# Moving sums to VectorE, norms half a group earlier and w_out blocks apart in the MLP stage of a fused attention, MoE and relu² kernel

## The chip, the cores and the metric

The kernel runs on one core of one Trainium2 chip. The metric is device time in microseconds of one execution, from the runs of a set. A NeuronCore has TensorE (PE; matmul), VectorE (DVE), ScalarE (ACT), GpSimd (POOL) and SyncE (SP), which each go through their instructions in order and meet at semaphores. PSUM holds what TensorE writes, SBUF the rest. [...]

## The reference

The kernel does three things one after the other, on 2304 tokens of 512 numbers: causal windowed attention with ALiBi, a top-1 mixture of experts, and an MLP whose activation is the square of relu. The change is in the third:

```python
def _moe2_ref(x, w_in, w_out):
    h = x @ w_in          # (2304, 512) @ (512, 2048)
    r = np.maximum(h, 0.0)
    g = r * r
    return (g @ w_out)    # (2304, 2048) @ (2048, 512)
```

## The kernel before

The last stage, `moe2`, begins at about 413 us. Its tokens are taken as they lie after the experts, in nine groups G of 256 (two tiles of 128 tokens). The output is put in the right order at the end, by an indirect scatter of each tile.

For a group there are three kinds of work.

- `norm(G)` scales the group's rows. It is a generator, so its steps can be placed between other work: ACT takes the absolute value (L1110), PE sums it (L1115), DVE makes the scale (L1118 to L1124), PE spreads it (L1129), DVE multiplies (L1130); then four differences of blocks of x (L1137 to L1140, on DVE for groups below 5, on POOL behind that) and the split of all blocks into two fp16 parts (casts L1150 on ACT, rests L1152 or L1156 on DVE). norm(G+2) is made while group G is at work.
- `wide1(G, m)` makes one half m of x @ w_in by a Strassen scheme: seven products of 24 matmuls (L1176). ACT takes the results out of PSUM (`keep`, L1188) and DVE joins them (L1189, L1221, L1223). `square(i)` makes relu² of them: on DVE for groups 0 to 2 (L1201), on ACT for 3 to 8 (L1204, L1205). `halves` splits a block of g into two fp16 parts, by a cast on ACT (L1195) and a subtraction on DVE (L1196).
- The product with w_out. Groups 0 to 2 are plain (SG = 3): `wide2(G, m)` takes 48 matmuls of 512 columns (L1351 to L1353) per half. Groups 3 to 8 use a Strassen scheme here as well: `seven(G, part)`, with products of 12 matmuls of 256 columns (L1307), eight in part 0 and six in part 1. It needs sums of blocks of g (L1208 and L1212 on POOL, L1214 and L1216 on DVE) and combined blocks of w_out.

Those combined blocks, for eight k, are made by `mix(k)`, which is a generator too. Its first call makes two sums (L1272) and four differences (L1274 to L1277) of a block on POOL, in scratch space: a column of `yT` that is free, or `dec`. Its second call splits them by ACT casts (L1281) and DVE (L1282). The table MIXES gives, at each of the points at(G, 0) to at(G, 4) between the halves, the blocks that begin or finish there: a block's first mention begins it, its second finishes it.

The order on each engine is made by a scheduler in the recording framework, which keeps to dependencies and to hints: `issue_after` puts what is recorded in it behind a given instruction, `behind` does so for one instruction. `end_act` and `end_dve` are the last `halves` of ACT and DVE. The outer loop is in `moe2`: wide2(G, 0) or seven(G, 0), wide1(G+1, 0), wide2(G, 1) or seven(G, 1), wide1(G+1, 1), with calls of `step()` (one step of norm(G+2)) and at(...) between.

In the profiled execution wide1(1,0) starts at 437.6 us, wide1(2,0) at 478.0, wide1(4,0) at 571.05, and seven(8,1), the last work, ends at 769.4.

Of the kernel before, what the change touches and what calls it, by code (L numbers as in the profile page):

```python
# [16 lines left out]
ALU = mybir.AluOpType  # L17
# [29 lines left out]
GT = 2  # L47
GW = GT * P
SG = 3
SCRATCH = {0: 0, 1: 1, 2: 1, 4: 3, 7: 4}  # L50
MIXES = {(0, 4): (0,), (0, 0): (1,), (0, 1): (0,), (0, 2): (1,), (1, 4): (2, 3), (1, 1): (2, 3),
         (2, 4): (4, 5), (2, 1): (4, 5), (2, 2): (7, 6), (2, 3): (7, 6)}
STEPS = (((2, 6), ()), ((1, 5), (1,)), ((4,), (1,)), ((1, 5), (1,)), ((1, 5), (1,)), ((3,), (1, 3)), ((3,), (1, 3)),
         ((1, 3, 5, 7), (1, 3)))
SPARE = ((), (), (4, 5, 6, 7), (4, 5, 6, 7), (4, 5, 6, 7), (6, 7), (7,), ())
# [38 lines left out]
class K:  # L94
    def __init__(self, ctx, tc, q, k, v, wg, w1, w2, wi, wo, cst, pad, out):
        self.ctx, self.tc, self.nc = ctx, tc, tc.nc
        self.q, self.k, self.v, self.wg, self.w1, self.w2, self.wi, self.wo, self.cst, self.pad, self.out = \
            q, k, v, wg, w1, w2, wi, wo, cst, pad, out
        self.cp = ctx.enter_context(tc.tile_pool(name="cp", bufs=1))
        self.wr = ctx.enter_context(tc.tile_pool(name="wr", bufs=12))  # L100
        self.rw = ctx.enter_context(tc.tile_pool(name="rw", bufs=4))
        self.ps = ctx.enter_context(tc.tile_pool(name="ps", bufs=2, space=PSUM))
        self.yp = ctx.enter_context(tc.tile_pool(name="yp", bufs=1))
        self.ep = ctx.enter_context(tc.tile_pool(name="ep", bufs=2))
        self.dr = ctx.enter_context(tc.tile_pool(name="dr", bufs=1, space=DRAM))
        self.xts, self.fac, self.gts = {}, {}, {}
        self.turns, self.narrow = 0, False
        self.wt = {}

        self.yT = self.yp.tile([P, 4, YC], F32, name="yT")  # L110
        self.xd = self.dr.tile([N, 2 * DM], F16, name="xd")
        self.ids = self.dr.tile([E * N + P, 2], F32, name="ids")
        self.cols = self.dr.tile([YC + P, 2], F32, name="cols")
        self.wod = self.dr.tile([P, 8 * 2 * DM], F16, name="wod")
# [1065 lines left out]
    def wide1(self, G, m, between=lambda k: None):  # L1180


        nc, V = self.nc, self.nc.vector
# [14 lines left out]
        def square(i):  # L1198
# [6 lines left out]
            nc.scalar.activation(ci, ci, AF.Square, scale=0.5)  # L1205
            both = lambda t: (t[:, a].rearrange("p (o j n) -> p o j n", o=2, j=4) for a in range(2))
            if i == 0:
                nc.gpsimd.tensor_tensor(p1, c[:, :, 0, 0], c[:, :, 0, 1], op=ALU.subtract)  # L1208
                halves(*(t[:, 0] for t in both(g[3])), c[:, :, 0, 0])
                halves(*(t[:, 1] for t in both(g[3])), p1)  # L1210
                return
            nc.gpsimd.tensor_tensor(p5, c[:, :, 0, 1], c[:, :, 1, 1], op=ALU.add)  # L1212
            halves(*(g[0][:, a].rearrange("p (j n) -> p j n", j=4) for a in range(2)), ci)
            V.tensor_tensor(u, p5, c[:, :, 0, 0], op=ALU.subtract)  # L1214
            halves(*both(g[1]), self.part(22528, 8 * P).rearrange("p (o j n) -> p o j n", o=2, j=4))
# [34 lines left out]
    def mix(self, k):  # L1250
# [10 lines left out]
            x = [pair(d[:, :512]), pair(d[:, 512:])]  # L1261
        if k < 2:
            y = [xg().bitcast(F16).rearrange("p (o a n) -> p o a n", o=2, a=2) for _ in range(2)]
        elif k < 6:
            col = column(k - 2).bitcast(F16).rearrange("p o (a n) -> p o a n", a=2)
            y = [col[:, 0:2], col[:, 2:4]]
        else:
            y = [self.wo_pair[f].rearrange("p (o a d) -> p o a d", o=2, a=2)[:, :, :, GW:] for f in (((0, 2), (4, 6))[k - 6])]
        self.wt[k] = [y[o // 2][:, o % 2] for o in range(4)]
        for o in range(2):  # L1270
            w = self.wo_s[8 * o + k]
            Q.tensor_tensor(x[o], *(w[:, a].rearrange("p (o n) -> p o n", o=2) for a in range(2)), op=ALU.add)  # L1272
        t1, t3, t4, t2 = (x[o // 2][:, o % 2] for o in range(4))
        Q.tensor_tensor(t1, t3, t1, op=ALU.subtract)  # L1274
        Q.tensor_tensor(t3, t2, t3, op=ALU.subtract)
# [54 lines left out]
    def put(self, G, i, o, src=None):  # L1330
        nc = self.nc
        if src is not None:
            self.end_act = nc.scalar.activation(o, src, AF.Copy, scale=self.fac[G][:, 1, i:i + 1])  # L1333
        k = G * GT + i
        nc.gpsimd.indirect_dma_start(  # L1335
            out=self.out, out_offset=bass.IndirectOffsetOnAxis(ap=self.oid[:, k:k + 1], axis=0),
            in_=o, in_offset=None)

    def wide2(self, G, m, then=lambda i: None):
        nc = self.nc  # L1340
# [19 lines left out]
    def moe2(self):  # L1360
# [15 lines left out]
        def at(*key):  # L1376
            for n in MIXES.get(key, ()):
                if n in mixing:
                    for _ in mixing.pop(n):
                        pass  # L1380
                else:
                    mixing[n] = self.mix(n)
                    next(mixing[n])

        mixing = {}
        for G in range(NG):
# [4 lines left out]
                with tc.issue_after(self.end_act.ins), tc.issue_after(self.end_dve.ins):  # L1391
                    next(nr)

            at(G, 4)
            if G < SG:
                self.wide2(G, 0)
            else:
                self.seven(G, 0, lambda k: step() if k in (5, 7) else None)
            at(G, 0)
            if more:  # L1400
                self.wide1(G + 1, 0, lambda k: step() if G >= SG and k < 2 else at(G, 1) if k == 1 else None)
            if G < SG:
                step()
                self.wide2(G, 1, lambda k: step() if k != 1 else None)
                if G + 1 == SG:
                    self.narrow = True
            else:
                self.seven(G, 1, lambda k: step() if k == 3 else None)
            at(G, 2)
            if more:  # L1410
                self.wide1(G + 1, 1, lambda k: step() if G >= SG and k == 0 else None)
# [61 lines left out]
```

## Time and profile before

| | us |
|---|---|
| three runs | 777.4, 782.7, 784.3 |
| median of them | 782.7 |
| the profiled execution | 782.7 |
| its span | 780.8 |
| busy in the span: PE | 718.3 (92%) |
| DVE | 592.3 (76%) |
| ACT | 443.3 (57%) |
| POOL | 236.2 (30%) |

The span is what the profiler recorded from first to last instruction; the execution's time has 1.9 us more around it. Busy time is the sum of an engine's instructions. A row of a timeline gives the start, the length, the engine, the line of the kernel, the operation, what it writes and reads, and in brackets how long its engine stood before it and what it waited for. A row of waits gives the instruction that waited, the one it waited for, the total, how often, and the longest.

### The profile page before, as it was taken

The page shows a single profiled execution, that of the slowest core. Times are in us where ns is not written, and L with a number is a line of the kernel's source. Part 1 is how long each engine was busy: PE and PEld are TensorE (multiplying, and loading weights), DVE is VectorE, ACT ScalarE, POOL GpSimd, SP SyncE. Part 2 cuts the span into 40 slices and gives each one's busy share as a digit, 9 for nine tenths or more (in the row PEclk, how much of TensorE's full clock was granted, in tenths as well). Part 3 has the DMA queues.
Part 4 walks back from the last instruction along what each step waited for, and adds up shares of the span by engine and source line. Part 5 has one row for each costly group of instructions (what it writes and reads, how often), then busy time and mean ns, then how long its engine had stood idle before and what let it go on. Part 6 is the DMA issues. An engine that isn't in the chain of part 4 may idle for free. (4 is left out here: it accounts for less than half of the span.)

```text
span 780.8 us, 19641 instructions
## 1 busy us (share of the span) xinstructions
PE 718.3 (92%) x7979; PEld 601.6 (77%) x7979; DVE 592.3 (76%) x1430; ACT 443.3 (57%) x748; POOL 236.2 (30%) x271
## 2 busy tenths in 40 slices
PE   6889999997979899998898999998799999999995
PEld 5889899787636566787797777675689898989994
DVE  5898889855679998887798987867567777777672
ACT  5878898733456565656533333336456565656561
POOL 4583421534632010000003453444622222222121
PEclk9999999999999999999899999999889999999998
DMA  9796215766789785476404000000000000000000
GB/s 339 275 387 151 65 56 135 240 173 158 244 292 299 239 258 172 153 244 223 155 31 138 1 29 2 28 2 28 1 2 29 2 29 3 29 2 29 2 29 28
DMA packets 35656, 91.71 MB, mean 117 GB/s; under 512 B 5209, under 2 KB 13547, under 8 KB 35547
## 3 DMA queue, kind: packets, MB, share of 16 engines
q1 hardware_dynamic: 29803, 75.77, 30.4%
q0 software_dynamic: 5760, 14.65, 5.7%
q8 instruction: 64, 1.05, 0.6%
q14 instruction: 29, 0.24, 0.1%
HBM read 77.54 MB, written 13.04 MB: 116 GB/s over the span
## 5 line engine op out<-in xcount | busy, mean ns | idle before, releaser
L1176 PEld LDWEIGHTS <-wi 128*128 128x128 f16 x3024 | 170.5, 98 | 8.8 <-issue 7.3
L1307 PEld LDWEIGHTS <-wr 128*128 128x128 f16 x1008 | 99.2, 99 | 20.1 <-ACT wr L1195 4.4
L1195 ACT CAST wr<-work 128x1024 f16<-128x1024 f32 (+1 forms) x72 | 59.9, 832 | 77.6 <-DVE work L1201 44.5
L1176 PE MATMUL ps_b<-work,wi 128*128 128x128 f16 x1368 | 85.5, 219 | 4.4 <-ACT work L1188 2.9
L1196 DVE TENSOR_TENSOR wr<-work,wr 128x1024 f16<-128x1024 f32 (+1 forms) x72 | 74.7, 1051 | 15.3 <-ACT wr L1195 13.1
L850 PE MATMUL ps_c<-work,wr 128*128 128x352 f16 (+5 forms) x256 | 75.0, 297 | 10.8 <-DVE work L799 9.8
L849 PE MATMUL ps_c<-work,wr 128*128 128x352 f16 (+5 forms) x256 | 75.0, 297 | 8.2 <-ACT yT L852 6.3
L1176 PE MATMUL ps_a<-work,wi 128*128 128x128 f16 x1248 | 78.2, 219 | 0.0
L851 PE MATMUL ps_c<-work,wr 128*128 128x352 f16 (+5 forms) x256 | 75.0, 297 | 0.0
L310 PE MATMUL ps_a<-yT,wr 128*128 128x192 f32 (+2 forms) x288 | 64.2, 342 | 6.8 <-DMA wr<-in_q_dram 5.2
L322 ACT ACTIVATE pb<-pb,nm 128x192 f32<-128x192 f32 (+2 forms) x144 | 56.1, 432 | 12.6 <-DVE nm L315 11.8
L770 DVE SCALAR_TENSOR_TENSOR wr<-rw,wr 128x1024 f16<-128x1024 f32 x40 | 48.7, 1220 | 6.4 <-ACT wr L769 6.4
L769 ACT ACTIVATE wr<-rw 128x1024 f16<-128x1024 f32 x40 | 42.1, 1057 | 19.1 <-DMA rw<-in_w_dram 18.6
L1272 POOL TENSOR_TENSOR yT<-wr 128x512 f32<-128x512 f16 x6 | 10.5, 1753 | 136.6 <-ACTq L1064 123.3
L310 PEld LDWEIGHTS ps_a<-yT,wr 128*128 128x128 f32 x288 | 45.0, 198 | 8.0 <-DMA yT<-in_k_dram 6.3
L315 DVE CUSTOM_DVE_ANT_0 pb<-ps_a,bias 128x192 f32<-128x192 f32 (+2 forms) x144 | 44.2, 326 | 8.8 <-PE ps_a L310 8.4
L1335 POOL DMA_INDIRECT out_dram<-o,oid x18 | 19.6, 1088 | 100.1 <-ACT o L1333 84.8
L851 PEld LDWEIGHTS <-wr 128*128 128x128 f16 x288 | 29.4, 102 | 21.5 <-issue 14.4
L1204 ACT ACTIVATE work<-work 128x1024 f32<-128x1024 f32 x24 | 25.3, 1055 | 34.0 <-DVE work L1189 34.0
L333 PE MATMUL ps_b<-cst,pb 128*128 128x128 f32 x256 | 43.7, 281 | 0.5 <-ACT pts L337 0.4
L850 PEld LDWEIGHTS <-wr 128*128 128x128 f16 x288 | 29.4, 102 | 17.6 <-issue 10.2
L778 POOL DMA_INDIRECT xg<-xd,idx x21 | 24.3, 1158 | 51.6 <-PE ps_d L786 40.8
(297 smaller groups left out, 1921.7 us busy)
## 6 DMA issues: line engine op xcount, KB each, us to landing
rw<-in_w_dram SPq DMA_DIRECT2D x40, 512.0 KB, 5.7
wi<-in_w_dram SPq DMA_DIRECT2D x20, 512.0 KB, 6.5
rw<-in_wo_dram SPq DMA_DIRECT2D x16, 512.0 KB, 3.9
rw<-in_wi_dram SPq DMA_DIRECT2D x32, 256.0 KB, 5.3
wr<-in_q_dram SPq DMA_DIRECT2D x14, 512.0 KB, 8.5
xd<-xhl POOLq DMA_DIRECT2D x16, 256.0 KB, 5.3
yT<-in_k_dram SPq DMA_DIRECT2D x7, 576.0 KB, 10.7
rw<-in_v_dram SPq DMA_DIRECT2D x12, 325.0 KB, 5.6
```

Of the source, the lines that this page charges most:

```text
L310: nc.tensor.matmul(ps[:, s, first:hi], q[g, u, hh // 4][:, hh % 4, s if u < 4 else 0, :], self.kt[g, hh // 2][:, hh % 2, key0:key0 + hi - ...
L315: self.last_ttr = nc.vector.tensor_tensor_reduce(out=pb[:, s, first:hi], in0=ps[:, s, first:hi], in1=self.bias[:, hh, first - lo:192], sca ...
L322: self.last_exp = nc.scalar.activation(pb[:, s, first:hi], pb[:, s, first:hi], AF.Exp, bias=nm[:, s:s + 1], scale=-1.0)
L333: nc.tensor.transpose(pt[:, t, :, s, :], pb[:, s, t * P:(t + 1) * P], self.idf)
L770: self.nc.vector.scalar_tensor_tensor(t[:, 1], st, sc, t[:, 0], op0=ALU.mult, op1=ALU.subtract)
L849: nc.tensor.matmul(py, wh, hh, start=fc == 0, stop=False)
L850: nc.tensor.matmul(py, wh, hl, start=False, stop=False)
L851: self.last_mm = nc.tensor.matmul(py, wl, hh, start=False, stop=fc == 7)
L1176: self.nc.tensor.matmul(ps[:, j], w[:, kp, a, w0 * P:(w0 + 1) * P], v[:, 2 * x + kp], start=kp + b == 0, stop=kp == 1 and b == 2)
L1195: self.end_act = nc.scalar.copy(hi, src)
L1196: self.end_dve = V.tensor_tensor(lo, src, hi, op=ALU.subtract)
L1307: nc.tensor.matmul(ps[n], x[:, v, j], y[j][:, w], start=m + i + j == 0, stop=m == 1 and i == 2 and j == 3)
```

## The change

It has five parts.

1. The sums of L1208 and L1212, twelve instructions each, go from POOL to DVE.
2. norm(G+2) of the plain groups (G below 3) takes its steps inside wide2(G, 0) instead of behind wide1(G+1, 0) and inside wide2(G, 1). In the later groups the steps inside seven are placed anew.
3. The table MIXES and its scratch space SCRATCH. Before, blocks 0 and 1 were made in group 0, 2 and 3 in group 1, and 4 to 7 in group 2, of which 6 and 7 ended at the change to the fourth group. Now the blocks begin one by one, and block 7 alone ends at that point. Block 6 lies in a column of yT.
4. The first sum of a `mix` goes behind `end_dve`.
5. The scatters of the output are declared independent of one another, since each writes other rows.

```diff
-SCRATCH = {0: 0, 1: 1, 2: 1, 4: 3, 7: 4}
...
+SCRATCH = {0: 0, 1: 1, 2: 1, 3: 2, 4: 3}
...
@@ wide1, square(i)
             if i == 0:
-                nc.gpsimd.tensor_tensor(p1, c[:, :, 0, 0], c[:, :, 0, 1], op=ALU.subtract)
+                V.tensor_tensor(p1, c[:, :, 0, 0], c[:, :, 0, 1], op=ALU.subtract)
...
-            nc.gpsimd.tensor_tensor(p5, c[:, :, 0, 1], c[:, :, 1, 1], op=ALU.add)
+            V.tensor_tensor(p5, c[:, :, 0, 1], c[:, :, 1, 1], op=ALU.add)
@@ mix
-        elif k < 6:
+        elif k < 7:
             col = column(k - 2).bitcast(F16).rearrange("p o (a n) -> p o a n", a=2)
...
-            Q.tensor_tensor(x[o], *(w[:, a].rearrange("p (o n) -> p o n", o=2) for a in range(2)), op=ALU.add)
+            sum_ = Q.tensor_tensor(x[o], *(w[:, a].rearrange("p (o n) -> p o n", o=2) for a in range(2)), op=ALU.add)
+            if o == 0:
+                self.behind(sum_, self.end_dve)
@@ put
-        nc.gpsimd.indirect_dma_start(
+        dma = nc.gpsimd.indirect_dma_start(
...
+        for old in self.outs:
+            self.tc.declare_no_dep(dma.ins, old.ins, reason="disjoint rows")
+        self.outs.append(dma)
@@ moe2
-            at(G, 4)
             if G < SG:
-                self.wide2(G, 0)
+                self.wide2(G, 0, lambda k: step())
             else:
-                self.seven(G, 0, lambda k: step() if k in (5, 7) else None)
+                self.seven(G, 0, lambda k: step() if k == 5 else None)
...
             if G < SG:
-                step()
-                self.wide2(G, 1, lambda k: step() if k != 1 else None)
+                self.wide2(G, 1)
...
-                self.seven(G, 1, lambda k: step() if k == 3 else None)
+                self.seven(G, 1, lambda k: step() if k in (0, 1) else None)
```

Lines behind the table move by a few numbers: L1274 to L1277 become L1276 to L1279, L1281 and L1282 become L1283 and L1284, L1293 and L1294 become L1295 and L1296, L1307 becomes L1309, L1333 and L1335 become L1335 and L1337.

What this does to the order is shown at three places. First DVE behind the division by the gate's sum (L736), which is the beginning of wide1(1,0). Before:

```order
L736 RECIPROCAL og<-ps_b 128x18
L1282 TENSOR_TENSOR xm<-yT,xm 128x2x256
L1165 SCALAR_TENSOR_TENSOR fac<-fac,og 128x2
L1282 TENSOR_TENSOR xm<-yT,xm 128x2x256
L1166 SCALAR_TENSOR_TENSOR fac<-fac 128x2
L1165 SCALAR_TENSOR_TENSOR fac<-fac,og 128x2
L1166 SCALAR_TENSOR_TENSOR fac<-fac 128x2
L1221 TENSOR_TENSOR work<-work 128x512
L1223 TENSOR_TENSOR work<-work 128x512
```

The change has there:

```order
L736 RECIPROCAL og<-ps_b 128x18
L1165 SCALAR_TENSOR_TENSOR fac<-fac,og 128x2 x2
L1166 SCALAR_TENSOR_TENSOR fac<-fac 128x2 x2
L1118 TENSOR_SCALAR fac<-ps_c 128x2
L1284 TENSOR_TENSOR xm<-yT,xm 128x2x256
L1119 TENSOR_SCALAR fac<-fac 128x2
L1284 TENSOR_TENSOR xm<-yT,xm 128x2x256
L1120 RECIPROCAL fac<-fac 128x2
L1124 TENSOR_SCALAR sd<-cst,fac 128x128 x2
L1165 SCALAR_TENSOR_TENSOR fac<-fac,og 128x2
L1166 SCALAR_TENSOR_TENSOR fac<-fac 128x2
```

The scale of norm(2) (L1118 to L1130) has come to this place, and the two splits of block 0, now L1284, stand between its L1118 and its L1120.

Second POOL from the beginning of the stage, where blocks 0 and 1 are made in columns of yT. Before:

```order
L1272 TENSOR_TENSOR yT<-wr 128x2x256 x2
L1274 TENSOR_TENSOR yT<-yT 128x256
L1275 TENSOR_TENSOR yT<-yT 128x256
L1276 TENSOR_TENSOR yT<-yT 128x256
L1277 TENSOR_TENSOR yT<-yT 128x256
L1272 TENSOR_TENSOR yT<-wr 128x2x256
L1274 TENSOR_TENSOR yT<-yT 128x256
L1272 TENSOR_TENSOR yT<-wr 128x2x256
L1275 TENSOR_TENSOR yT<-yT 128x256
L1276 TENSOR_TENSOR yT<-yT 128x256
L1277 TENSOR_TENSOR yT<-yT 128x256
L1335 DMA out_dram<-o,oid 2304x512 x2
```

With the change:

```order
L1272 TENSOR_TENSOR yT<-wr 128x2x256 x3
L1276 TENSOR_TENSOR yT<-yT 128x256
L1272 TENSOR_TENSOR yT<-wr 128x2x256
L1277 TENSOR_TENSOR yT<-yT 128x256
L1276 TENSOR_TENSOR yT<-yT 128x256
L1278 TENSOR_TENSOR yT<-yT 128x256
L1277 TENSOR_TENSOR yT<-yT 128x256
L1279 TENSOR_TENSOR yT<-yT 128x256
L1278 TENSOR_TENSOR yT<-yT 128x256
L1279 TENSOR_TENSOR yT<-yT 128x256
L1337 DMA out_dram<-o,oid 2304x512 x2
```

Before, block 0 had six operations in a row (two sums, four differences) and block 1 came as a piece of its own; now the two are interleaved, and the last difference of block 0 is the first L1279, the tenth operation.

Third ACT from the last `halves` of wide1(4,0) to the keeps of wide1(4,1). Before:

```order
L1195 CAST wr<-work 128x1024 x2
L1195 CAST wr<-work 128x512
L1294 ACTIVATE o<-o,fac 128x256
L1333 ACTIVATE o<-o,fac 128x512
L1150 CAST work<-yT 128x512
L1150 CAST work<-yT 128x256
L1150 CAST work<-dec 128x1024
L1188 ACTIVATE work<-ps_b 128x512
L1188 ACTIVATE work<-ps_a 128x512
```

With the change:

```order
L1195 CAST wr<-work 128x1024 x2
L1195 CAST wr<-work 128x512
L1150 CAST work<-yT 128x512
L1150 CAST work<-yT 128x256
L1150 CAST work<-dec 128x1024
L1296 ACTIVATE o<-o,fac 128x256
L1335 ACTIVATE o<-o,fac 128x512
L1188 ACTIVATE work<-ps_b 128x512
L1188 ACTIVATE work<-ps_a 128x512
```

The three casts L1150 of norm(5) stand behind the scaling of the output before, and ahead of it now.

## Rows read from the trace of the kernel before

**Rows 1.** Stretches: us; busy us of PE, PEld, DVE, ACT, POOL; PEclk; DMA share.

```profile
437.60:571.05 133.45, 124.27 (x1383) 91.38 (x1382) 99.04 (x137) 56.51 (x79) 59.19 (x51) 0.96 0.04 13
561.60:570.40 8.80, 7.21 (x33) 4.58 (x34) 6.91 (x10) 5.47 (x9) 0.21 (x1) 0.50 0.01 2
222.00:225.80 3.80, 3.51 (x12) 1.65 (x12) 0.70 (x2) 0.66 (x2) 0.00 (x0) 0.55 1.02 324
```

**Rows 2.** Waits of PE from 413 us on: total us, times, longest.

```profile
PE ps_d L1307 <- ACT wr L1195: 4.2, 1, 4.2
PE ps_b L1176 <- ACT work L1188: 2.9, 4, 0.7
PE ps_c L1115 <- ACT dec L1110: 2.5, 1, 2.5
PE ps_a L1115 <- ACT dec L1110: 2.4, 4, 0.7
PE ps_b L1129 <- DVE sd L1124: 2.0, 1, 2.0
...
PE ps_d L1307 <- ACT wr L1281: 1.3, 1, 1.3
```

**Rows 3.** Lines L1272 and L1276 on POOL: ns min/median/max, first and last start.

```profile
L1272 POOL TENSOR_TENSOR yT<-wr x6: 1147/1536/3472, 414.1 to 466.4; 128x512 f32<-128x512 f16 x6
...
L1276 POOL TENSOR_TENSOR yT<-yT x5: 727/730/1707, 418.7 to 549.0; 128x256 f32<-128x256 f32 x5
```

**Rows 4.** Timeline of POOL (start, us, what, idle before and releaser), at 433.

```profile
433.53 3.47 POOL L1272 TENSOR_TENSOR yT<-wr 128x512 f32<-128x512 f16 x1 [13.22 <-DVE work L1152]
```

**Rows 5.** Timeline of DVE, at 419, 433, 438 and 492.

```profile
419.65 1.21 DVE L1221 TENSOR_TENSOR work<-work 128x512 f32<-128x512 f32 x1
...
433.30 1.22 DVE L1196 TENSOR_TENSOR wr<-work,wr 128x1024 f16<-128x1024 f32 x1
...
438.09 0.68 DVE L1282 TENSOR_TENSOR xm<-yT,xm 128x512 f16<-128x512 f32 x1
...
492.15 1.23 DVE L1196 TENSOR_TENSOR wr<-work,wr 128x1024 f16<-128x1024 f32 x1 [1.11 <-ACT wr L1195]
...
494.19 0.48 DVE L1124 TENSOR_SCALAR sd<-cst,fac 128x128 bf16<-128x128 f32 x2
```

**Rows 6.** Timeline of PE: starts of wide1(1,0), wide1(2,0), and a product's wait.

```profile
437.39 0.38 PE L1353 MATMUL ps_d<-wr 128*128 128x512 f16 x1
437.61 1.50 PE L1176 MATMUL ps_c<-work,wi 128*128 128x128 f16 x24
...
477.99 1.50 PE L1176 MATMUL ps_a<-work,wi 128*128 128x128 f16 x24
...
594.65 1.50 PE L1176 MATMUL ps_b<-work,wi 128*128 128x128 f16 x24 [0.73 <-ACT work L1188]
595.99 1.50 PE L1176 MATMUL ps_a<-work,wi 128*128 128x128 f16 x24
```

**Rows 7.** Timeline of ACT between wide1(4,0) and wide1(4,1), 588 to 595.

```profile
588.82 0.62 ACT L1195 CAST wr<-work 128x512 f16<-128x512 f32 x1 [0.69 <-DVE work L1216]
...
593.07 1.04 ACT L1150 CAST work<-dec 128x1024 f16<-128x1024 f32 x1
594.02 0.58 ACT L1188 ACTIVATE work<-ps_b 128x512 f32<-128x512 f32 x1
```

**Rows 8.** Lines L1212 (POOL) and L1214 (DVE), and idle before L1214.

```profile
L1212 POOL TENSOR_TENSOR work<-work x12: 1265/1268/1275, 532.3 to 758.1; 128x512 f32<-128x512 f32 x12
...
L1214 DVE TENSOR_TENSOR work<-work x12: 691/692/693, 533.7 to 759.4; 128x512 f32<-128x512 f32 x12
...
  POOL work L1212: 28.5, 12
```

**Rows 9.** Timeline of POOL: two of the gathers, and the last scatter.

```profile
234.85 1.81 POOL L778 DMA_INDIRECT xg<-xd,idx  x1 [0.30 <-issue]
...
774.82 0.98 POOL L1335 DMA_INDIRECT out_dram<-o,oid  x1 [2.54 <-DMA out_dram<-o,oid]
```

More of the change, by code (lines that the diff above doesn't have):

```diff
@@ L49 @@
 SG = 3
-SCRATCH = {0: 0, 1: 1, 2: 1, 4: 3, 7: 4}
-MIXES = {(0, 4): (0,), (0, 0): (1,), (0, 1): (0,), (0, 2): (1,), (1, 4): (2, 3), (1, 1): (2, 3),
-         (2, 4): (4, 5), (2, 1): (4, 5), (2, 2): (7, 6), (2, 3): (7, 6)}
+SCRATCH = {0: 0, 1: 1, 2: 1, 3: 2, 4: 3}
+MIXES = {(0, 0): (0,), (0, 1): (0, 1), (0, 2): (1, 2), (0, 3): (2, 3), (1, 0): (3, 4), (1, 2): (4, 5),
+         (1, 3): (5,), (2, 0): (6,), (2, 2): (6, 7), (2, 3): (7,)}
 STEPS = (((2, 6), ()), ((1, 5), (1,)), ((4,), (1,)), ((1, 5), (1,)), ((1, 5), (1,)), ((3,), (1, 3)), ((3,), (1, 3)),
@@ L107, in __init__ @@
         self.turns, self.narrow = 0, False
-        self.wt = {}
+        self.wt, self.outs = {}, []
         self.yT = self.yp.tile([P, 4, YC], F32, name="yT")
@@ L1267, in mix @@
         else:
-            y = [self.wo_pair[f].rearrange("p (o a d) -> p o a d", o=2, a=2)[:, :, :, GW:] for f in (((0, 2), (4, 6))[k - 6])]
+            y = [self.wo_pair[f].rearrange("p (o a d) -> p o a d", o=2, a=2)[:, :, :, GW:] for f in (0, 2)]
         self.wt[k] = [y[o // 2][:, o % 2] for o in range(4)]
```

## The prediction, on record before the changed kernel ran

> **What bounds the kernel now.** I read the table of stretches first, because the change touches only the last stage, the relu² MLP. From 571.05 us on TensorE (PE) is the bound, with short waits; the stretch before that is where PE stands. In 437.60 to 571.05 PE is busy 124.27 of 133.45 us, so it stands 9.2 us [rows 1]. It also loses time while it works: from 561.60 to 570.40 its granted clock is 0.50, the lower of its two levels, so 7.21 us of busy time cost about 3.6 more than at full clock [rows 1]. Together 12.8 us are lost in this stretch.
>
> Second I read the waits of PE [rows 2]. The reader is to see four things. At the change from the third group to the fourth PE waits 4.2, 1.3 and 0.2 us for `halves` and casts. The 2.5 us are one wait of L1115, the norm's first step, for L1110 in wide2(2,1). The four waits of 0.7 for L1188 are one in each later group, 2.9 in all. The L1115 row of 2.4 us holds four waits; three of them, 0.65 each, stand one in each steady group that still has a norm to make (groups 4 to 6), the fourth earlier.
>
> Third I read single engines. L1272 to L1277 (sums and differences of one w_out block) on POOL take 1.15 us for a sum and 0.73 for a difference at best, and up to 3.47 and 1.71 [rows 3]. The 3.47 us one started at 433.53, beside L1196 and what follows it on DVE [rows 4, 5].
>
> **Places of the sum.** The profiled execution took 782.7 us, as does the median of the three runs, so the sum goes by 782.7.
>
> *Start of the second group (wide1(1,0)).* This is what the change costs most. PE now reaches L1129 of norm(2) after 21 matmuls of the first product. The product starts at 437.61; eight small matmuls of L1115 take 0.2 and 21 matmuls 1.2, so PE is there at 439.0 [rows 6]. L1129 waits for DVE's L1124. On DVE the two splits of block 0 (L1284, before L1282) now stand between L1118 and L1120, and DVE goes in order. The second split waits for ACT's cast and that for the tenth operation of POOL, the last difference of block 0. Of the ten only the first can run early; the second is the sum that the edit puts "behind" the last `halves`, and that L1196 ends at 434.5 [rows 5]. So three sums and six differences lie between 434.5 and L1129. The first sum runs beside DVE's L1152s, so I put it halfway between 1.15 and 3.47, 2.3 us. Then DVE stands still, and the others go at their fast rows: two sums at 1.15, six differences at 0.73, each with about 0.1 between. That is 2.4 + 2.5 + 5.0 = 9.9, so POOL is done at 444.4. Behind it come a cast (0.6, an estimate from the 1.04 of one twice as large), the split 0.68, L1120 some 0.2 and L1124 0.48 [rows 5, 7]: 446.4. PE stands 7.4 us. After a single long wait of PE that ended at 222 the clock was 0.55 for 3.8 us, so 3.51 us of work cost 1.6 more [rows 1]; I add the same 1.6. Cost 9.0. With the fast row for the first sum as well, POOL is done at 443.2 and PE stands 6.3; with the slowest rows for all nine (3.47 and 1.71, and the gaps) POOL needs 21.6 and PE stands 19.1. These are the two bounds, 7.9 and 20.7 with the clock. I stay by the fast side since DVE, the other user in the slow rows, is waiting here.
>
> [...]
>
> *Second group (wide2(1,0)).* L1115 of norm(3) now stands after about 35 matmuls of wide2(1,0). By the undisturbed chain of wide1(2,0), PE starts at 477.99 and the last L1196 ends at 493.4, so the chain needs 15.4 us from its first matmul [rows 5, 6]. Behind it come two more splits of a block (2 x 0.68) and L1110, a pass over 128x1024 (1.04, as the cast of that size) [rows 5, 7]: 17.8. PE gets there after seven products of 1.34 and 35 matmuls of 0.216, 16.9 [rows 6]. So 0.9 us is missing even undisturbed. POOL makes another block beside it, and L1221 beside POOL took 1.21 us where the same sum alone takes 0.69 [rows 5, 8]; with two or three such delays I take 2.2, and 1.0 more at L1129, which has only five matmuls in front of it against the four operations from L1118 to L1124. Cost 3.2, bounds 0.9 and 5 (eight such delays).
>
> *Third group (wide2(2,0)).* The same place, with the block's splits out of the way: the chain's 15.4 and L1110 end before PE's 16.9, so what remains is the run from L1118 to L1124 against five matmuls and a little of block 6; 1.4, bounds 0 and 2.5. The 2.5 us wait of before, which is this step half a group later, goes.
>
> *Change of groups (seven(3,0)).* Three of the four blocks that were made in the last half group are made earlier, only block 7 is left. In a steady group the last L1195, at 588.82, ends 18.4 us after the start at 571.05, and the casts and splits of block 7 (4 in all, beside each other, 1.3 to 2) stand behind it: first results at 19.0, last at 20.4 [rows 1, 7]. PE is at their first use after 9.4 of wide1 and some 78 matmuls of 256 columns at half of 0.216, 17.8. So 1.2 to 2.6 are missing, and the clock may fall a little; I take 2.4, bounds 0.5 and 3.5, in place of 4.2 + 1.3 + 0.2 and the slow clock of 3.6.
>
> After: 9.0 + 3.2 + 1.4 + 2.4 = 16.0. Before: 12.8. The stretch gets **3.2 us longer**.
>
> *Steady groups.* L1188 at 594.02 starts where the L1150 casts end, and PE's product at 594.65 waits 0.73 for it [rows 6, 7]. In the changed order of ACT the casts stand ahead of L1296 and L1335, and the differences that feed them are finished half a group sooner, so this wait goes: **-2.9** in four groups. L1115 now follows three products of the next half, so its three waits of 0.65 go: **-1.95**. The 24 sums cost 1.27 us on POOL and will cost 0.69 on DVE, as the same sum of L1214 does [rows 8]. DVE gets 16.6 us of work, of which PE's products hide all as long as `halves` are done before w_out starts; POOL's sum stood 0.6 us per sum longer in the chain, so there the move gains a little. I put it at nothing. If the cover is gone, each group gets up to two sums, 1.4 us, later.
>
> *Start of the stage.* Block 0's differences no longer run beside DVE at 419.65, where L1221 took 1.21 us for the 0.69 of such a sum; PE waits 2.0 us for the chain behind it (L1124) [rows 2, 5, 8]. **-0.5**; 0 if the loads decide.
>
> *Tail.* The last scatter starts at 774.82 and waits 2.54 for the write of the one before [rows 9]. Without the order it can start as back-to-back gathers do, with 0.30 of idle time between [rows 9], so 2.2 sooner. **-2.1**, 0.1 left for the queue; 0 if the two writes go one after the other in the queue all the same. The other pairs end beside PE.
>
> Sum: 782.7 + 3.2 - 2.9 - 1.95 - 0.5 - 2.1 = **778.4 us**.
>
> **Rivals.**
>
> *A: the stall is small and the rest clean.* POOL runs all nine operations fast (7.9 with the clock), and the chains of groups 1 to 3 are ready when PE comes. For it: with DVE waiting nothing disturbs POOL, and spreading takes the load from DVE at the change. Against: by the undisturbed rows group 1 is 0.9 short. Then 7.9 in place of 12.8, 4.9 less: 782.7 - 4.9 - 7.45 = 770.3 us.
>
> *B: the waits of the steady groups come back.* 24 more operations stand on an in-order DVE; L1208 stands between two joins, and L1212 waits for ACT's L1205 with L1214 behind it. If this makes the last `halves` 1 to 2 us late, the 2.9 and some 1 of the L1115 waits stay: 782.3 us. Against it: DVE sat idle 28.5 us before the twelve L1214, 2.4 each, waiting for POOL [rows 8].
>
> *C: slower.* POOL's nine operations at wide1(1,0) run at their slow rows. For it: the 3.47 us row is this very sum at this very place [rows 4]. Against: what ran beside it then waits now. Price: with 20.7 in place of 9.0, 778.4 + 11.7 = 790.1 us. It becomes slower than before once the idle time there is over 7.4 + 4.3 = 11.7 us, as it is if the differences take 1.45 us each.
>
> **How the numbers follow.** A measurement of this kernel can tell about 1% from no change, that is 774.8 and 790.5. My forecast (774 to 783) has 0.47, A 0.31 (767 to 774), B 0.11, C 0.11 (784 to 797). Faster than 774.8: A and the edge of the forecast, 0.36. Slower than 790.5: somewhat over half of C, 0.07. Same: the rest, 0.57. The range 769.5 to 786 leaves out the lower part of A, 0.09, and most of C, 0.10.
>
> **What would show it.** In the new profile: one wait of L1129 for L1124 at about 439 us, of 6 to 9 us, with a granted clock near 0.5 behind it; POOL with nine operations without a gap up to 444; waits of one to three us for L1115 in wide2(1,0) and wide2(2,0); a wait of 1 to 3.5 at about 566 where 5.8 stood; no L1188 or L1115 waits in groups 4 to 7; the last two scatters 1.3 us apart. I am wrong if L1129 waits less than 5 or more than 12, if the L1188 waits stay, or if PE waits for `halves` of L1196 behind the new sums.

## The result: 770.6 us, 1.4% faster

The changed kernel takes 770.64 us (median of four runs, 769.61 to 771.1) against 782.65 (777.44 to 784.3). The ratio is 0.986, with an interval of 0.981 to 0.990. The forecast was 778.4 us and no change beyond 1%. The time is inside the stated range and at the number that rival A gave, but it came about another way, as the experiments show.

The span fell from 780.8 to 767.5 us, by 13.3. The first question is where. These are the four parts of the last stage in the profile of the changed kernel (columns as in [rows 1]): from the third product of wide1(0,0) to wide1(1,0), from there to wide1(4,0), to wide1(8,0), to the end.

```profile
412.30:434.03 21.73, 20.84 (x235) 14.77 (x235) 18.82 (x34) 8.23 (x12) 3.80 (x3) 1.00 0.35 123
434.03:565.90 131.87, 122.67 (x1367) 91.74 (x1366) 98.41 (x140) 56.63 (x80) 53.63 (x52) 0.97 0.04 13
565.90:715.55 149.65, 149.65 (x2058) 141.98 (x2056) 119.63 (x200) 95.48 (x127) 28.78 (x24) 1.00 0.05 16
715.55:767.50 51.95, 45.13 (x578) 42.13 (x575) 27.81 (x45) 22.69 (x30) 3.99 (x4) 0.96 0.06 22
```

The kernel before has 22.46, 133.44, 155.84 and 53.91 us for the same four (415.15 to 437.61, 571.05, 726.89 and 780.80). The third of them, the steady groups, in which PE is busy for 150.97 of 155.84 us before and without a break now:

```profile
571.05:726.89 155.84, 150.97 (x2054) 141.50 (x2051) 112.71 (x183) 94.66 (x126) 41.76 (x40) 1.00 0.04 15
```

So the parts give -0.7, -1.6, -6.2 and -2.0, together -10.5. The other 2.85 us lie ahead of the first of these points, where no engine's order of work differs. In the eleven runs below that point lies between 408.5 and 415.8 us, and two runs of one and the same kernel have 408.5 and 415.5. So it is a draw: it changes from run to run without an edit, and lengths from that point on are the sharper comparison.

What PE waits for from 405 us on in the changed kernel:

```profile
PE ps_a L1129 <- DVE sd L1124: 6.5, 1, 6.5
PE ps_b L1176 <- DVEq L1064: 1.4, 1, 1.4
PE ps_b L1129 <- DVE sd L1124: 1.4, 2, 0.9
PE ps_a L1115 <- ACT dec L1110: 0.8, 1, 0.8
PE ps_b L1115 <- ACT dec L1110: 0.7, 1, 0.7
PE ps_d L1309 <- DVE wr L1284: 0.6, 1, 0.6
```

Of [rows 2] little is left: no wait for L1188, no wait of L1115 in the steady groups, and 0.6 us at the change of groups where 4.2, 1.3 and 0.2 stood. L1115 waits 0.8 and 0.7 us, in wide2(1,0) and wide2(2,0). One long wait is new: L1129 waits 6.5 us for L1124. That is the wait which the prediction put at 7.4. Its chain on POOL and DVE:

```profile
430.64 3.52 POOL L1272 TENSOR_TENSOR yT<-wr 128x512 f32<-128x512 f16 x2 [17.93 <-DVE wr L1196]
434.11 0.74 POOL L1276 TENSOR_TENSOR yT<-yT 128x256 f32<-128x256 f32 x1
434.80 1.16 POOL L1272 TENSOR_TENSOR yT<-wr 128x512 f32<-128x512 f16 x1
...
437.95 1.18 POOL L1277 TENSOR_TENSOR yT<-yT 128x256 f32<-128x256 f32 x1
439.10 0.72 POOL L1279 TENSOR_TENSOR yT<-yT 128x256 f32<-128x256 f32 x1
```

```profile
434.16 0.15 DVE L1118 TENSOR_SCALAR fac<-ps_c 128x2 f32<-128x2 f32 x1
437.32 1.23 DVE L1284 TENSOR_TENSOR xm<-yT,xm 128x512 f16<-128x512 f32 x1 [3.01 <-ACT xm L1283]
...
440.50 0.69 DVE L1284 TENSOR_TENSOR xm<-yT,xm 128x512 f16<-128x512 f32 x1 [1.34 <-ACT xm L1283]
441.11 0.16 DVE L1120 RECIPROCAL fac<-fac 128x2 f32<-128x2 f32 x1
441.30 0.75 DVE L1124 TENSOR_SCALAR sd<-cst,fac 128x128 bf16<-128x128 f32 x2
```

The nine operations of POOL begin at 430.64, right behind the L1196 that they were put behind, and the ninth (L1279 at 439.10) ends at 439.8: 9.2 us for the forecast 9.9. DVE stands 3.01 and 1.34 us in front of its two L1284 and lets L1124 go only at 441.3. Behind the wait the clock is low:

```profile
441.90:446.90 5.00, 4.99 (x53) 4.99 (x53) 4.57 (x11) 2.12 (x4) 0.00 (x0) 0.56 0.00 0
```

This is the granted clock of TensorE, PEclk in the rows; in the traces of both kernels it has two values, 1.00 and 0.50, and 0.56 is the mean of this stretch. A product of 24 matmuls takes 2.77 us there (from 442.39) and 1.50 behind it (from 446.94). By the mean, 4.99 us of work cost 2.2 more than at 1.00, an estimate. By the whole length of wide1(1,0) (18.28 us for 9.38 of products and 0.1 of small matmuls) wait and clock cost 8.8 us; the forecast was 9.0.

In the steady groups, the sums are on DVE, and ACT's casts stand ahead of the output's scaling, as the order had it:

```profile
L1212 DVE TENSOR_TENSOR work<-work x12: 691/692/693, 539.2 to 746.1; 128x512 f32<-128x512 f32 x12
```

```profile
584.08 0.62 ACT L1195 CAST wr<-work 128x512 f16<-128x512 f32 x1 [0.69 <-DVE work L1216]
...
585.43 1.04 ACT L1150 CAST work<-dec 128x1024 f16<-128x1024 f32 x1
...
587.40 0.57 ACT L1188 ACTIVATE work<-ps_b 128x512 f32<-128x512 f32 x1
```

L1188 starts 21.5 us behind the group's start at 565.90; before, at 594.02, it was 23.0 behind 571.05 [rows 7]. The last two scatters are 1.6 us apart, for the wait of 2.54 in [rows 9]:

```profile
759.95 0.97 POOL L1337 DMA_INDIRECT out_dram<-o,oid  x1 [21.63 <-ACT o L1335]
761.56 0.97 POOL L1337 DMA_INDIRECT out_dram<-o,oid  x1 [0.64 <-DVE o L1328]
```

### The profile page after: what moved, and what is told of

Same layout as the page of the kernel before. It is cut to its first block, busy times and chain, and to the rows that moved or that the text cites. A ratio compares the mean times of both kernels' runs of the same rounds, so it can differ in the third digit from the quotient of the medians.

```text
span 767.5 us, 19611 instructions
## 1 busy us (share of the span) xinstructions
PE 715.7 (93%) x7979; PEld 603.0 (79%) x7979; DVE 595.9 (78%) x1454; ACT 444.2 (58%) x748; POOL 210.4 (27%) x247
## 5 line engine op out<-in xcount | busy, mean ns | idle before, releaser
L1176 PEld LDWEIGHTS <-wi 128*128 128x128 f16 x3024 | 172.7, 98 | 11.0 <-issue 9.3
L1309 PEld LDWEIGHTS <-wr 128*128 128x128 f16 x1008 | 98.1, 98 | 12.3 <-issue 1.0
L1195 ACT CAST wr<-work 128x1024 f16<-128x1024 f32 (+1 forms) x72 | 59.9, 832 | 59.2 <-DVE work L1201 42.4
L1176 PE MATMUL ps_a<-work,wi 128*128 128x128 f16 x1344 | 84.9, 220 | 0.0
L1176 PE MATMUL ps_b<-work,wi 128*128 128x128 f16 x1272 | 80.0, 220 | 1.4 <-DVEq L1064 1.4
L1196 DVE TENSOR_TENSOR wr<-work,wr 128x1024 f16<-128x1024 f32 (+1 forms) x72 | 68.9, 980 | 4.4 <-ACT wr L1195 4.4
L1337 POOL DMA_INDIRECT out_dram<-o,oid x18 | 25.4, 1412 | 122.1 <-ACT o L1335 87.5
L1272 POOL TENSOR_TENSOR yT<-wr 128x512 f32<-128x512 f16 x8 | 11.4, 1430 | 144.6 <-ACTq L1064 120.0
L778 POOL DMA_INDIRECT xg<-xd,idx x21 | 26.6, 1265 | 49.6 <-PE ps_d L786 42.4
```

The lines of the kernel that those rows point to most:

```text
L1176: self.nc.tensor.matmul(ps[:, j], w[:, kp, a, w0 * P:(w0 + 1) * P], v[:, 2 * x + kp], start=kp + b == 0, stop=kp == 1 and b == 2)
L1195: self.end_act = nc.scalar.copy(hi, src)
L1196: self.end_dve = V.tensor_tensor(lo, src, hi, op=ALU.subtract)
L1309: nc.tensor.matmul(ps[n], x[:, v, j], y[j][:, w], start=m + i + j == 0, stop=m == 1 and i == 2 and j == 3)
```

## The experiments

In the text, "the last stage" is the length from the third product of wide1(0,0) to the end, from the profile of a run; the median of the times stands beside it. The first column differs by up to 1.5 us between two profiles of one kernel.

| kernel | to wide1(1,0) | to wide1(4,0) | to wide1(8,0) | to the end | last stage | median time |
|---|---|---|---|---|---|---|
| before | 22.5 | 133.4 | 155.8 | 53.9 | 365.7 | 781.0 to 782.7 |
| changed | 21.7 | 131.9 | 149.7 | 52.0 | 355.2 | 770.6 |
| changed, again | 22.4 | 131.9 | 149.7 | 52.0 | 355.8 | 771.2 |
| changed, scatters in order | 22.0 | 132.0 | 149.7 | 53.8 | 357.5 | 772.0 |
| changed, sums on POOL | 22.0 | 133.0 | 156.4 | 52.0 | 363.3 | 778.2 |
| changed, late norm as before | 21.9 | 132.9 | 149.5 | 52.0 | 356.2 | 770.8 |
| changed, plain norm as before | 21.3 | 134.2 | 149.7 | 52.3 | 357.4 | 770.0 |
| changed, block 0 early | 22.9 | 129.1 | 149.7 | 52.3 | 353.8 | 768.2 |
| same, block 1 later | 24.1 | 127.3 | 149.7 | 52.0 | 353.1 | 767.1 |
| same, block 1 behind norm(2) | 22.8 | 123.8 | 149.7 | 52.0 | 348.3 | 762.0 |
| before, sums on DVE | 23.9 | 127.6 | 149.5 | 54.4 | 355.3 | 766.0 |
| the same, again | 22.4 | 127.6 | 149.4 | 54.4 | 353.9 | 767.4 |
| before, sums on DVE and independent scatters | 22.5 | 127.6 | 149.4 | 52.4 | 351.9 | 766.9 |

**The change again.** No edit.

> The changed kernel once more, on the chip and in the rounds of the three that follow. First theory (the change itself gives about 10.5 us behind the start of the last stage, and 2.7 us of the first comparison lay ahead of every changed instruction): 770 to 774 us, and the place of the first product of wide1(0,0) behind the experts differs from the profile before by run, not by kernel. Rival (the change also shortens the stages ahead): that place is again 2.5 to 3 us earlier than in the profile before.

Measured: 771.15 us, ratio 0.987 (0.984 to 0.989) with 17 runs of before at 781.48. The third product started at 413.26, 1 us later than in the first profile, and the last stage took 355.8. The first theory holds: the change is worth about 10 us behind that point. That the point itself is a draw is shown by the two sets of the sums alone, below.

**The sums back on POOL.**

```diff
-                V.tensor_tensor(p1, c[:, :, 0, 0], c[:, :, 0, 1], op=ALU.subtract)
+                nc.gpsimd.tensor_tensor(p1, c[:, :, 0, 0], c[:, :, 0, 1], op=ALU.subtract)
...
-            V.tensor_tensor(p5, c[:, :, 0, 1], c[:, :, 1, 1], op=ALU.add)
+            nc.gpsimd.tensor_tensor(p5, c[:, :, 0, 1], c[:, :, 1, 1], op=ALU.add)
```

> The changed kernel with the sums L1208 and L1212 back on GpSimd, all else kept. First theory (the steady groups got shorter by the norm's steps, not by the sums): the steady groups stay within 0.5 us of 37.4, the time within 2 us of the changed kernel. Rival (the sums on VectorE are what ends the waits of the steady groups): each group gets 0.9 to 1.8 us longer, 4 to 7 us in all.

Measured: 778.23 us, 7.1 above the change; ratio to before 0.995 (0.993 to 0.997). The rival is right and the prediction's view of the steady groups falls. The waits of PE in this run:

```profile
PE ps_b L1176 <- ACT work L1188: 2.8, 4, 0.7
...
PE ps_d L1309 <- DVE wr L1196: 1.4, 5, 0.3
```

The four waits for L1188 are back at 0.7 each, as in [rows 2], though the casts L1150 and the norm's steps stand at their new places. The four groups take 156.4 us, no less than the 155.8 of before.

The trace shows that the new places and the sums on POOL work against each other. By the new places the norm's four differences (L1137 to L1140, on POOL in these groups) run later, and L1208 now stands right behind them. It starts 12.3 us behind wide1(4,0) at 570.77, where the kernel before has 10.0, and ACT waits for it:

```profile
583.05 1.26 POOL L1208 TENSOR_TENSOR work<-work 128x512 f32<-128x512 f32 x1
```

```profile
584.34 0.62 ACT L1195 CAST wr<-work 128x512 f16<-128x512 f32 x1 [2.93 <-POOL work L1208]
```

From the last L1195 to L1188 it is then 3.4 us (590.85 to 594.28) instead of 5.2 [rows 7]: the new place of L1150 gains 1.8 us there, and the later L1208 loses 2.3.

**The late groups' norm at its old places.**

```diff
-                self.seven(G, 0, lambda k: step() if k == 5 else None)
+                self.seven(G, 0, lambda k: step() if k in (5, 7) else None)
...
-                self.seven(G, 1, lambda k: step() if k in (0, 1) else None)
+                self.seven(G, 1, lambda k: step() if k == 3 else None)
```

> The changed kernel with the norm's steps of the later groups (group 3 on) back at their old places in seven, all else kept. First theory (these places carry the gain of the steady groups): the waits for L1188 and L1115 come back, the groups take 38.5 to 39.2 us instead of 37.4, the time is 4 to 6.5 us above the changed kernel. Rival (the sums on VectorE carry it): the groups stay below 37.9 and the time within 2 us.

Measured: 770.79 us, ratio 0.987 (0.984 to 0.990), the same as the change. No L1188 and no L1115 wait came back, and the four groups take 149.45 us.

Together the two runs are clear: with the sums on DVE the groups take 149.5 us with either placing of the norm, and with the sums on POOL 156 us with either.

**The sums alone.** The kernel before with L1208 and L1212 on DVE (the edit above, the other way round), measured in two sets.

> The kernel before with one part of the change alone: L1208 and L1212 on VectorE. Theory after the run with the sums back on GpSimd: the steady groups take 37.4 to 37.7 us instead of 39.2 (6 to 7 us in four), and at the change to the fourth group the 4.2 us wait for the halves goes too, since no sum stands behind blocks on GpSimd any more, so 8 to 11 us below the kernel before. Rival (the sums give their gain only together with the spread blocks): the wait at the change stays and the gain is at most 6 us.

> The kernel before with the sums on VectorE alone, a second time. Its first time (766 us) was 4 to 5 us below what its last stage accounts for, with the stages ahead ending at 408.5 us where other runs had 410 to 416. If that was the draw of those runs: the median is 768 to 772 us here and the last stage starts at 411 to 416. If these stages are shorter in this kernel for a reason that the order does not show: 764 to 767 us again, start below 410. In both cases the last stage itself takes 355 us.

Measured: 765.95 us (ratio 0.981, 0.978 to 0.985) and 767.37 (0.981, 0.977 to 0.985). One part of the change alone is faster than the whole of it. The first theory holds for the last stage, which is 10.4 and 11.8 us shorter than before; the medians are 15.1 and 14.0 us lower, more than it said. The four groups take 149.4 us, and the waits at the change to the fourth group shrink as well:

```profile
PE ps_d L1307 <- ACT wr L1281: 2.0, 1, 2.0
...
PE ps_c L1115 <- ACT dec L1110: 0.9, 1, 0.9
PE ps_d L1307 <- DVE wr L1196: 0.9, 1, 0.9
PE ps_d L1307 <- ACT wr L1195: 0.6, 1, 0.6
```

The 4.2 us for L1195 are 0.6, the 2.5 of L1115 0.9; the 1.3 for L1281 grow to 2.0. The stretch to wide1(4,0) gets 5.8 us shorter. In the kernel before, L1208 of wide1(3,1) stood behind two blocks of w_out in POOL's queue, and ACT waited for it:

```profile
556.51 1.26 POOL L1208 TENSOR_TENSOR work<-work 128x512 f32<-128x512 f32 x1
```

```profile
557.81 0.62 ACT L1195 CAST wr<-work 128x512 f16<-128x512 f32 x1 [4.29 <-POOL work L1208]
```

The last stage took 355.3 and 353.9 us. Of the two guesses about the draw neither fits in full: the last stage started at 408.5 us in the first set and at 415.5 in the second, so the start is a draw, and yet the medians are alike, and 3 to 5 us below the change, whose last stage is no more than 2 us longer. The twelve runs spread over 762 to 771 us. What sets the length of the stages ahead is open.

**The scatters in order again.** The loop that declares them independent is taken out of the changed kernel.

```diff
-        for old in self.outs:
-            self.tc.declare_no_dep(dma.ins, old.ins, reason="disjoint rows")
```

> The changed kernel with the scatters of the output ordered one behind the other again. Theory of the prediction: the second of the last pair starts 3.5 us behind the first instead of 1.3, the end is 2.1 us later, nothing else moves: 773 us. Rival (the two writes go one after the other in the queue in any case): within 0.5 us at the end of the last stage.

Measured: 771.99 us, ratio 0.989 (0.986 to 0.992). In the profile the last two scatters are 3.50 us apart again and wide1(8,0) to the end takes 53.8 us for the change's 52.0. The theory holds in the trace; in the medians 0.8 us cannot be told from none.

**Sums and scatters on the kernel before.** Both edits, the sums on DVE and the independent scatters, and nothing else of the change.

> The kernel before with two parts of the change: the sums on VectorE and the scatters independent. Theory: the parts add up, so the last scatter starts 1.6 us behind the one before instead of 3.5 and the end of the kernel is 1.9 us below the run with the sums alone; its last stage takes 353.4 us. Rival (the scatters need the rest of the change): no difference at the end.

Measured: 766.94 us, ratio 0.981 (0.976 to 0.985). The last stage takes 351.9 us, 2.0 below the second set of the sums alone, as the theory said (its 353.4 started from the first set), and 1.97 us of the gain lie behind wide1(8,0) (52.42 for 54.39). The medians of the two kernels, 766.9 and 767.4, don't resolve it. Against the whole change (355.2 and 355.8) the last stage is 3.3 to 3.9 us shorter: that is what the other three parts (the norm's places, table, `behind`) cost together.

**The plain groups' norm at its old places.**

```diff
-                self.wide2(G, 0, lambda k: step())
+                self.wide2(G, 0)
...
-                self.wide2(G, 1)
+                step()
+                self.wide2(G, 1, lambda k: step() if k != 1 else None)
```

> The changed kernel with the norm's steps of the plain groups back at their old places, all else kept. First theory (moving these steps is what puts the nine operations of GpSimd in front of L1129): the wait at the start of wide1(1,0) and its slow clock go (8.8 us), the old waits of 0.4, 0.5 and 2.5 us for L1115 come back in place of 1.3, 0.8: 5 to 7.5 us below the changed kernel, 764 to 766 us. Rival (the stall moves to the first products with w_out, which wait for the late block): within 2 us of the changed kernel.

In this run block 4 uses column 3 of yT as scratch before norm(3) has read it, so the x of group 3 is replaced by other numbers; the work is the same. Measured: 769.99 us, ratio 0.986 (0.984 to 0.989), 1 us below the change. The rival is right on the time: the wait of 6.5 is gone, but others took its place, at L1115 and not at the products with w_out that it named.

```profile
PE ps_a L1115 <- ACT dec L1110: 3.5, 1, 3.5
PE ps_b L1115 <- ACT dec L1110: 2.7, 1, 2.7
```

The last stage took 357.4 us, 1.6 to 2.2 more than the change's. For the first of these waits, in wide2(0,1), the trace shows the reason. It is POOL's nine operations again, by way of ACT, on which the first `keep` of wide1(1,0) stands behind the second cast of block 0:

```profile
439.45 0.62 ACT L1283 CAST xm<-yT 128x512 f16<-128x512 f32 x1 [2.58 <-POOL yT L1279]
439.98 0.59 ACT L1188 ACTIVATE work<-ps_c 128x512 f32<-128x512 f32 x1
```

That L1188 starts 6.75 us behind the start of wide1(1,0) at 433.23; in the kernel before it is 1.6. L1110, at the end of the same chain, ends 18.2 us behind that start instead of 15.1. So the old places of the norm don't remove the stall with this table, they move it on. The wait of 2.7 was not followed.

**Block 0 early.** In the changed kernel block 0 is no longer put behind `end_dve`, so POOL makes it at the start of the stage, as before.

```diff
-            if o == 0:
+            if o == 0 and k > 0:
                 self.behind(sum_, self.end_dve)
```

> The changed kernel with block 0 let go from the end of the last halves, so that GpSimd makes it at the start of the stage as before; all other blocks keep that order. First theory (the wait of L1129 at the start of wide1(1,0), 6.5 us and some 2 us of slow clock behind it, hangs on the nine operations of GpSimd): the wait falls to 0 to 1.5 us, no slow clock follows, and the time is 6 to 8.5 us below the changed kernel, about 763 us. Rival (block 1, which still starts there, and the splits hold DVE just as long): the wait stays above 4 us and the time within 3 us of the changed kernel.

Measured: 768.17 us, ratio 0.982 (0.978 to 0.986). The gain of 3 us lies between the theories: the wait fell only to 2.8 us, and a slow clock did follow, of 3.0 us by an estimate (wide1(1,0) takes 15.32 us; the wait, 9.38 of products and 0.1 of small matmuls leave that much). The reason for the wait stands on DVE:

```profile
435.38 1.38 DVE L1284 TENSOR_TENSOR xm<-yT,xm 128x512 f16<-128x512 f32 x1
436.69 1.10 DVE L1165 SCALAR_TENSOR_TENSOR fac<-fac,og 128x2 f32<-128x2 f32 x1
437.71 0.68 DVE L1284 TENSOR_TENSOR xm<-yT,xm 128x512 f16<-128x512 f32 x1
...
439.10 0.71 DVE L1119 TENSOR_SCALAR fac<-fac 128x2 uint32<-128x2 uint32 x1
...
440.04 0.82 DVE L1124 TENSOR_SCALAR sd<-cst,fac 128x128 bf16<-128x128 f32 x2
```

```profile
433.81 3.96 POOL L1272 TENSOR_TENSOR yT<-wr 128x512 f32<-128x512 f16 x2 [14.29 <-DVE wr L1196]
```

Block 1 still starts behind L1196, and its two sums (3.96 us for two that take 1.15 each at best) run beside DVE's work in front of L1129. L1165, two numbers a partition, takes 1.10 us, and L1119 0.71; with POOL standing they take 0.15 and 0.17 (last run below).

**Block 1 later.** The run before, and block 1 begun at (0, 2), behind wide1(1,0); blocks 2 to 4 half a step later.

```diff
-MIXES = {(0, 0): (0,), (0, 1): (0, 1), (0, 2): (1, 2), (0, 3): (2, 3), (1, 0): (3, 4), (1, 2): (4, 5),
+MIXES = {(0, 0): (0,), (0, 1): (0,), (0, 2): (1,), (0, 3): (1, 2), (1, 0): (2, 3), (1, 1): (3, 4), (1, 2): (4, 5),
```

> The run with block 0 early, and besides block 1 begun only behind wide1(1,0) (blocks 2 to 4 half a step later as well). Theory: in that run L1129 still waited 2.8 us because block 1 on GpSimd ran beside the short DVE operations in front of it (L1165 1.10 us, L1119 0.71); with GpSimd still there, L1129 waits at most 0.5 us, the clock stays at 1.00, and wide1(1,0) takes 9.5 to 10.2 us up to the next product instead of 18.1 and 15.3: 5 to 6 us below the run with block 0 early, 762 to 764 us. Rival (a later block shifts the load into the second and third group): waits of more than 2 us appear in wide2(1,0) or at the change to the fourth group and the gain is under 3 us.

Measured: 767.10 us, ratio 0.984 (0.981 to 0.986). The theory is right on wide1(1,0), the rival on the time, 1.1 us below the run before. L1129 at wide1(1,0) has no wait any more, and wide1(1,0) takes 9.5 us, but in wide2(2,0), one group later than the rival said, this stands:

```profile
517.87 0.35 PE L1115 MATMUL ps_b<-onesb,dec 128*128 128x1 bf16 x8 [3.00 <-ACT dec L1110]
```

```profile
514.08 1.13 ACT L1283 CAST yT<-dec 128x512 f16<-128x512 f32 x2
516.67 1.06 ACT L1110 ACTIVATE dec<-yT 128x1024 bf16<-128x1024 f32 x1 [1.46 <-DVE yT L1284]
```

```profile
515.35 1.29 DVE L1284 TENSOR_TENSOR yT<-dec,yT 128x512 f16<-128x512 f32 x2
```

A block in `dec` is now split right there, and L1110, which writes `dec`, waits for the splits L1284 that read it.

**Block 1 behind norm(2).** Block 0 early, and block 1 behind the last difference of the norm (L1140) instead of the last halves; the table is the changed kernel's.

```diff
-        Q.tensor_tensor(t4, b[:, 1, 0], t2, op=ALU.subtract)
+        self.end_norm = Q.tensor_tensor(t4, b[:, 1, 0], t2, op=ALU.subtract)
...
-            if o == 0:
-                self.behind(sum_, self.end_dve)
+            if o == 0 and k > 0:
+                self.behind(sum_, self.end_norm if k == 1 else self.end_dve)
```

> The changed kernel with block 0 made at the start of the stage, and block 1 behind the last difference of norm(2) on VectorE instead of behind the last halves; all later blocks as in the changed kernel. Theory (GpSimd beside the short operations of VectorE in front of L1129 is what was left of the wait, 2.8 us; the later places are untouched): L1129 waits at most 0.5 us with the clock at 1.00, the waits of wide2(1,0), wide2(2,0) and of the change stay at 0.8 and 0.5, 0.8, 0.6, and the stretch from wide1(0,0)'s third product to wide1(4,0) is 146 to 148 us (154.2 in the changed kernel): 762 to 764 us. Rival (block 1 is late for the next point as in the run with block 1 half a step later): a wait of over 2 us in wide2(2,0), at best 767.

Measured: 762.04 us (759.93 to 763.98), ratio 0.975 (0.971 to 0.979). It beats both kernels. Its median is 9 us below the change; 6.9 to 7.5 of them are in the last stage, where the cause is shown. The theory holds number for number; the stretch to wide1(4,0) from the third product is 22.8 + 123.8 = 146.6 us, and the waits behind the start of the stage are, besides 0.5 at L1129 in wide2(1,0),

```profile
PE ps_a L1115 <- ACT dec L1110: 0.8, 1, 0.8
PE ps_b L1115 <- ACT dec L1110: 0.7, 1, 0.7
PE ps_d L1309 <- DVE wr L1284: 0.6, 1, 0.6
PE ps_a L1129 <- DVE sd L1124: 0.5, 1, 0.5
```

```profile
432.44:556.25 123.81, 120.66 (x1367) 89.71 (x1366) 97.53 (x140) 55.16 (x78) 51.81 (x47) 1.00 0.04 14
```

with the clock at 1.00, where the change had 0.97.

## Why the prediction was right and wrong

*Start of wide1(1,0): right.* Forecast 9.0 us, measured 8.8: the wait 6.5 for 7.4, the slow clock 2.2 for 1.6. The cause is shown by the last run above, in which the POOL work is moved and the wait is 0.5. That the price of the clock came so near is in part luck: it was taken from one stretch at 222 us, and with block 0 early it was 3.0 behind a wait of only 2.8. The choice of POOL's fast rows "since DVE, the other user in the slow rows, is waiting here" held: of the nine operations those beside a standing DVE took 0.72 to 0.74 and 1.16 us. Beside the first L1284 one of the two engines was slow each time: L1278 took 0.73 and L1284 1.23, then L1277 1.18.

The sums of POOL show the difference as well: in the changed kernel one took 1.16 us with DVE standing, and two took 3.52 beside L1152 and what follows it on DVE. The run with block 0 early shows that DVE's side is hit too: L1165 took 1.10 us beside POOL's sums, and 0.15 with POOL standing in the last run.

*Second and third group, change of groups: right in kind, too dear.* The forecast was 3.2, 1.4 and 2.4 us. From the lengths of the pieces (12.41 for wide2(1,0), 11.73 for wide2(2,0), 11.47 for seven(3,0), against 10.36 or 10.5 and some 0.3 of small matmuls in the first two) they cost about 1.7, 1.1 and 1.0. Together that is 3.2 us of the miss. For wide2(1,0) the step that failed is the allowance for delays by POOL ("two or three such delays I take 2.2"): the wait there is 0.8, near the lower bound of 0.9, and the one at L1129 0.5 for 1.0. At the change of groups the first split was ready 19.0 us behind the start of wide1(3,1), as forecast, but PE came to it at 18.4 and not at 17.8, the last split ended at 19.6 for the forecast 20.4, and the clock stayed at 1.00.

*The stretch before: too low.* I took 12.8 us of loss from idle time and clock; by the pieces' lengths the old stretch had about 13.9, since a wait also leaves a part that no row counts as idle (in a steady group 0.16 us: the half with the wait of 0.73 is 10.27 us long, without it 9.38). That is 1.1 us of the miss. In sum the stretch became 1.6 us shorter where I had forecast 3.2 longer.

*Steady groups: right that the waits go, wrong why.* Forecast -4.85, measured -6.2. The step that failed is "I put it at nothing", said of the sums. I saw that POOL's sums lengthen their chain by 0.6 us each, and gave that no price; but the chain ends at the L1188 for which PE waits. In the kernel with the sums alone L1188 starts 22.0 us behind wide1(4,0) instead of 23.0, and the wait of 0.73 is gone, though the norm and the output's scaling stand where they did. The reason that I gave, the new place of L1150 in ACT's order, is not needed for that, and does not end the waits by itself: with the sums on POOL, L1150 was in its new place and the waits of 0.7 stayed. It has a worth of 1.8 us there, which the later L1208 takes back. For the other half of my reason was wrong: the differences are not "finished half a group sooner". They end 12.8 us behind wide1(4,0) in the changed kernel, and 8.9 before. The size of a wait in the waits view (0.73) was also smaller than what the half gained by its going (0.89).

*Tail: right.* -2.1 forecast, -2.0 measured, and shown by two runs.

*Start of the stage: right.* -0.5 forecast, -0.7 in the first profile and -0.1 in the second; the wait of L1129 is 0.8 to 1.5 us in every run in which POOL leaves block 0 for later, and 1.9 to 2.0 in every run in which it makes it there.

*Rivals.* A had the number, 770.3, with a stall of 7.9 us and no others. The stall was 8.8 and others of 3.8 stood; what made up for them was 1.1 us of old losses that A had not counted, 1.3 us in the groups and a draw of 2.85 us ahead of the stage. So that A met the time is luck. B did not come: L1208 and L1212 on DVE wait for ACT 4.2 and 9.2 us in all, and PE waits for none of it. C did not come.

*The sum.* In the profile the forecast is 8.8 us too high: 3.2 and 0.2 of costs after, 1.1 of losses before, 1.3 in the steady groups, 0.1 in the small terms together, and 2.85 of the draw. By the two sets the forecast of no change beyond 1% was wrong: both ratios lie below 0.99 at nearly all of their interval. In the last stage the whole gain is one part of the change, the sums; the scatters give 2 us more, and the remaining parts together take 3 to 4 us back.

## What to carry to other kernels

Cost a moved instruction by the chain it stands in and by what stands ahead of it in its engine's queue, not by its engine's share: 0.6 us saved on each sum were worth 6 us in the steady groups, and nearly 6 more were won in the stretch before, where a sum had stood behind other work on POOL. Before two parts of a change are credited with one gain, run each alone; here one part was better alone than with the others. When a wait hangs on another engine's burst, look for a place a few microseconds later, behind a named instruction that must not wait; here that place was worth some 7 us of the last stage.

## What the runs showed of the hardware

The operations of DVE that were slow beside POOL lost 0.3 to 1 us each in the rows read here, a short one as much as a long one, so that by proportion the short ones lost most. With block 0 early L1165, a pass over two numbers a partition, took 1.10 us and L1119 0.71, where they took 0.15 and 0.17 with POOL standing, in the run with block 1 behind norm(2); L1284, over 512 numbers, took 1.38 and 0.68; two L1124 took 0.82 and, in the later run, 0.48. In the kernel before, L1221, over 512 numbers, took 1.64 beside two sums of POOL and 0.69 alone:

```profile
463.76 1.64 DVE L1221 TENSOR_TENSOR work<-work 128x512 f32<-128x512 f32 x1
...
481.50 0.69 DVE L1221 TENSOR_TENSOR work<-work 128x512 f32<-128x512 f32 x1 [2.04 <-ACT work L1188]
```

```profile
463.25 3.16 POOL L1272 TENSOR_TENSOR dec<-wr 128x512 f32<-128x512 f16 x2
```

And a wait of PE does not fix the clock behind it: after the same wait of 1.98 us for L1129 the next products ran at full clock in the kernel before (1.50 us for 24 matmuls), while in the first run of the sums alone one of them took 2.76 us:

```profile
417.71 0.22 PE L1129 MATMUL ps_b<-sd,onesb 128*128 128x128 bf16 x1 [1.98 <-DVE sd L1124]
...
419.02 2.76 PE L1176 MATMUL ps_a<-work,wi 128*128 128x128 f16 x24
```

That run has 23.9 us in the first column of the table; the second set of the same kernel, with 1.50 for that product behind a wait of 1.93, has 22.4. What makes the column 24.1 with block 1 later is not shown here. After waits of 2.8 (block 0 early) and of 6.5 us (the change) at the start of wide1(1,0), the two kernels lost about the same to the clock, by estimate 3.0 and 2.2 us. What decides this is not settled here.
